# Second product of a fused feed-forward layer on four 32-row tiles of the tensor engine instead of the whole array

## The chip, the core and the metric

The kernel runs on one core of one Trainium2 chip. The core has a tensor engine (PE) with a queue of its own for instructions, a vector engine (DVE), a scalar engine (ACT), a general engine (POOL) and a sync engine (SP) that issues transfers; sixteen DMA engines carry the transfers. Matmuls write into eight banks of PSUM, each 128 partitions by 512 float32; DVE and ACT move results from there to SBUF. The metric is the device time of the program in microseconds (us), lower is better.

## What is computed

Attention with 32 learned queries, then attention of all tokens back to those 32 vectors, then a feed-forward layer with a leaky activation. B = 4 batches, N = 12480 tokens each, C = 128, m = 32, 2048 hidden units, 49920 tokens in all.

```python
def _attn_ref(x, inducing):
    B, N, C = x.shape                      # (4, 12480, 128)
    scale = 1.0 / np.sqrt(C)
    I = np.broadcast_to(inducing[None], (B, m, C))
    def mab(q, kv):
        s = scale * (q @ kv.transpose(0, 2, 1))
        a = np.exp(s - s.max(-1, keepdims=True))
        a /= a.sum(-1, keepdims=True) + 1e-09
        return a @ kv
    h = mab(I, x)                          # (B, 32, 128)
    return mab(x, h)

def _moe_ref(x, w_in, w_out, alpha):       # x: (49920, 128), d_ff = 2048
    h = x @ w_in
    g = np.maximum(h, 0.0) + alpha * np.minimum(h, 0.0)
    return g @ w_out
```

## The kernel before

**Algebra.** The output of the second attention is a weighted mean of the 32 rows of h, so the kernel never forms it. For each batch it makes hW = h times w_in (32 by 2048) once, and the hidden layer of a token is its 32 exponentials times hW, without the denominator, which is positive and goes through the activation. The leaky activation is split: g = relu(.) (1 - alpha) + alpha (.), so the output is relu(e hW) times W1 plus e times hA, with W1 = (1 - alpha) w_out and hA = h (w_in alpha w_out), 32 by 128. The division by the sum of exponentials comes last.

**Tiling.** A batch has six supertiles of 2048 tokens and a rest of 192. A supertile has four groups of 512 tokens; a batch has NG = 25 groups, the last of 192 tokens. For a group, the exponentials `rep` stand as 32 rows by 512 tokens, copied four times down the 128 partitions.

**A step of the main loop (L796-802).** A group has four steps j. `fill` (L443) makes four chunks of 128 hidden units: four matmuls of 32 rows each (`rep`, `hW`), one on each quarter of the array's rows, into four banks of the ring. ACT or DVE then reads each bank, takes the relu and writes it as bf16 to `gt` (L466, L468); which engine takes which bank is settled beforehand by a search, `make_plan` (L724). Then `mm2` (L473) of the step before adds its four chunks into the group's accumulator: four matmuls over all 128 rows with weights `W1`. There are two accumulators and a ring of six banks. `linear` (L497) adds e times hA with one more 32-row matmul for each group. `finish` (L507) turns a finished accumulator with DVE (L516), scales it by the denominators on POOL (L518) and stores it with four transfers from POOL's queue (L531), of the last groups from SP's. Every instruction of an engine is pinned to the order in which the program gives it (`pin`, L57).

**What is woven in.** `tasks` holds, by group and step, the work of the same batch's next supertile and of the next batch: `b_scores` (the exponentials of a supertile: four matmuls, one exp on ACT, a store to DRAM from SP), `b_rep` (four loads from SP that copy them), `b_den` and `b_turn` (denominators); for the next batch `a_load` (x by POOL's queue), `a_xpose` (a transposing transfer from SP, three groups later), `a_scores` (five groups after the load) and `a_accum` (eight groups after), one supertile every two groups; and at the batch's end `h_sum`, `h_den`, `h_transpose`, `h_weights` and `h_linear`. All of it uses banks of the ring. `h_weights` makes hW as 32 rows by 512 columns in four column quarters, and one DVE instruction moves it.

Of the kernel before, what the change touches and what calls it, by code (L numbers as in the profile page):

```python
# [16 lines left out]
P = 128  # L17
# [4 lines left out]
RING = 6  # L22
# [3 lines left out]
def kernel(  # L26
# [47 lines left out]
    xn_pool = ctx.enter_context(tc.tile_pool(name="xnp", bufs=8))  # L74
    xt_pool = ctx.enter_context(tc.tile_pool(name="xtp", bufs=2))
    gt_pool = ctx.enter_context(tc.tile_pool(name="gtp", bufs=4))
    head_pool = ctx.enter_context(tc.tile_pool(name="headp", bufs=3))
    rd_pool = ctx.enter_context(tc.tile_pool(name="rdp", bufs=3))
# [8 lines left out]
    )  # L87
    ring = [psum.tile([P, GRP], f32, name=f"ring{i}") for i in range(RING)]
    accs = [psum.tile([P, GRP], f32, name=f"acc{i}") for i in range(2)]
    ring_n = [0]  # L90

    def bank():
        t = ring[ring_n[0] % RING]
        ring_n[0] += 1
        return t
# [8 lines left out]
    def new_batch(b):  # L104
        st = Batch()
        st.b = b
        st.xT = xt_pool.tile([C, NS, NQ, GRP], bf16, name="xT", tag="xT")
        st.xTr = xt_pool.tile([C, JR, PR], bf16, name="xTr", tag="xTr")
        st.xn = {}
        st.e1T = {}  # L110
        st.sc = scale
        st.rs = None
        st.e2 = {}
        st.d = {}
        st.rep = {}
        st.rden = {}
        st.rt = {}
        if b > 0:
            st.es = work.tile([P, NS + 1], f32, name="es", tag="es")
            st.hacc = work.tile([P, C], f32, name="hacc", tag="hacc")  # L120
            nc.vector.memset(st.es[:], 0.0)
            nc.vector.memset(st.hacc[:], 0.0)
        return st

# [18 lines left out]
    def a_xpose(st, u):  # L143
        xn = st.xn[u]
        if u < NS:
            pin(nc.sync.dma_start_transpose(  # L146
                out=st.xT[:, u, :, :].rearrange("c q (j p) -> c (q j) p", j=NB),
# [8 lines left out]
    def p_xpose(st, u, i, last=False):  # L156
        xn = st.xn[u]
        if u == NS:
            tp = bank()[:].bitcast(bf16)
# [6 lines left out]
            ))  # L166
            return
        cut = 2 if last else 1
        for h in range(cut):
            tp = bank()[:].bitcast(bf16)  # L170
# [7 lines left out]
            dst = st.xT[:, u, qs[0] : qs[-1] + 1, :].rearrange("c q t -> c (q t)")  # L178
            w = len(qs) * GRP
            if h == 0:  # L180
                pin(nc.vector.tensor_copy(out=dst, in_=tp[:, :w]))  # L181
            else:
                pin(nc.scalar.copy(out=dst, in_=tp[:, :w]))

    def p_blocks(st, u, i):
        if u == NS:
            return [(st.xTr[:, j, :], st.xn[u][:, j, :]) for j in range(JR)]
        return [
            (st.xT[:, u, q, j * P : (j + 1) * P], st.xn[u][:, q, j * C : (j + 1) * C])
# [3 lines left out]
    def p_scores(st, u, i):  # L193
# [9 lines left out]
        ))  # L203
        st.e1T[u, i] = e1t
# [20 lines left out]
    def warm(st, n=1):  # L225
        for _ in range(n):
            mm(
                accs[0][:, P:], ident[:],
                st.xT[:, 0, 0, : 3 * P], start=False, stop=False, skip_group_check=True,
# [7 lines left out]
    def p_scale(st, et):  # L237
# [4 lines left out]
        pin(nc.vector.reciprocal(out=st.rs[:], in_=ps[:, 0:1]))  # L242

# [22 lines left out]
    def a_scores(st, u):  # L266
        ps = bank()
        if u < NS:
            for q in range(NQ):
                mm(ps[32 * q : 32 * q + 32, :], IT[:], st.xT[:, u, q, :])  # L270
# [3 lines left out]
            ))  # L274
            e1T = work.tile([P, NB, P], bf16, name="e1T", tag="e1T")
            pin(nc.sync.dma_start_transpose(out=e1T[:], in_=e1[:]))
        else:
# [5 lines left out]
            ))  # L283
            e1T = work.tile([P, JR, M], bf16, name="e1Tr", tag="e1Tr")
# [5 lines left out]
    def a_accum(st, u):  # L290
# [3 lines left out]
        if u < NS:  # L294
# [10 lines left out]
            ))  # L305
        else:
# [7 lines left out]
            ))  # L314

# [5 lines left out]
    def h_den(st):  # L321
# [5 lines left out]
        pin(nc.vector.tensor_scalar_mul(out=st.fr[:], in0=fold[:], scalar1=rh[:]))  # L327


    def h_transpose(st):  # L330
# [3 lines left out]
        pin(nc.vector.tensor_copy(out=st.hT4[:], in_=ps[:, :P]))  # L334
        st.hT = st.hT4[:, 0:M]

    def h_weights(st, first=False):
        ps = bank()
        for r in range(4):
            mm(  # L340
                ps[32 * r : 32 * r + 32, :], st.hT,
                w_in_b[:, r * NJ * P : (r + 1) * NJ * P],
            )
        st.hW = work.tile([P, NJ, P], bf16, name="hW", tag="hW")

        for j0, j1 in ((0, 1), (1, NJ)) if first else ((0, NJ),):
            evac_h(
                st, st.hW[:, j0:j1, :].rearrange("m j k -> m (j k)"), ps[:, j0 * P : j1 * P]
            )

    def h_linear(st):
# [3 lines left out]
        evac_h(st, st.hA[:], pa[:, :C])  # L355


    def tokens_of(st, s, q):
        return st.xT[:, s].rearrange("c j (q p) -> c j q p", q=NQ)[:, :, q, :]
# [4 lines left out]
    def b_scores(st, s):  # L364
# [14 lines left out]

        nq = NQ if s < NS else 1  # L380
# [14 lines left out]
    def b_scores_pe(st, q):  # L395
# [7 lines left out]
        ))  # L403
        st.rep[q] = st.rep0[:, q, :]

    def b_den(st, s):
# [11 lines left out]
        ))  # L418
        rt = dram.tile([pp, n, nq], f32, name="rt", tag="rt" if s < NS else "rtr")
# [15 lines left out]

    held = []

    def flush():
        while held:
            finish(*held.pop())  # L440

    def fill(st, g, j):
        pp, nb, cp = shape_of(g)  # L443
        t = pp * nb
        w = t * cp
        rep = st.rep[g]
        gt = gt_pool.tile([P, 4, GRP], bf16, name="gt", tag="gt")
        banks = []
        for r in range(4):
            ps = bank()  # L450
            for i in range(cp):
                mm(
                    ps[:, i * t : (i + 1) * t],
                    st.hW[32 * r : 32 * r + 32, j * cp + i, :],
                    rep[32 * r : 32 * r + 32, :t],
                )
            banks.append(ps)
        lin = j == NJ // cp - 1 and lin_groups(st.b, g)
        if lin:
            linear(st, lin)  # L460
        bits, pos = plan[st.b * NG + g, j]
        for r, ps in enumerate(banks):
            if r == pos:
                flush()
            if bits >> r & 1:
                pin(nc.scalar.activation(out=gt[:, r, :w], in_=ps[:, :w], func=RELU))  # L466
            else:
                pin(nc.vector.tensor_relu(gt[:, r, :w], ps[:, :w]))  # L468
        flush()
        return gt  # L470

    def mm2(st, g, j, gt):
        pp, nb, cp = shape_of(g)  # L473
        t = pp * nb
        acc = accs[(st.b * NG + g) % 2]
        begun = (g % 2 == 1 and st.b + g > 1) or cp > 1
        for r in range(4):
            for i in range(cp):
                c = r * NJ + j * cp + i
                mm(  # L480
                    acc[:, :t], W1[:, c, :], gt[:, r, i * t : (i + 1) * t],
                    start=(j == 0 and r == 0 and i == 0 and not begun),
                    stop=False, skip_group_check=True,
                )
        if j == NJ // cp - 1 and st.b * NG + g > 0:
            held.append((st, g))

    def lin_groups(b, g):
        if g % 2 == 0 and (b, g) != (0, 0):
            return [g, g + 1] if g + 1 < NS * NQ else [g]
        return []

    def linear(st, groups):
        for r, g in enumerate(groups):  # L497
            pp, nb, cp = shape_of(g)
            t = pp * nb
            mm(  # L500
                accs[(st.b * NG + g) % 2][:, :t], st.hA[32 * r : 32 * r + 32, :],
                st.rep[g][32 * r : 32 * r + 32, :t],
                start=(r == 1 or cp > 1), stop=False, skip_group_check=True,
            )

    def finish(st, g):
        pp, nb, _ = shape_of(g)  # L507
        t = pp * nb
        acc = accs[(st.b * NG + g) % 2]
# [6 lines left out]
        pin(nc.vector.transpose(out=ot[:, :t], in_=acc[:, :t]))  # L516
        ob = ob_pool.tile([P, GRP], f32, name="ob", tag="ob")
# [5 lines left out]
        t0 = st.b * N + s * SUP  # L523
# [312 lines left out]
```

## Time and profile before

| what | value |
|---|---|
| median of 3 runs (lowest, highest) | 590.22 us (589.33, 590.91) |
| the profiled execution, its own time | 591.21 us |
| its span | 589.4 us |
| granted tensor engine clock, mean over the span | 0.992 |
| PE busy (matmuls) | 558.5 us, 95% |
| DVE busy | 517.6 us, 88% |
| ACT busy | 502.0 us, 85% |
| POOL busy | 384.8 us, 65% |
| first `fill` of the main loop starts | 25.1 us |
| first turn of an accumulator (L516) | 38.9 us |
| last turn of an accumulator | 580.95 us |

The profile is one execution, on its own clock from the span's start. A row of groups names a line, an engine, an operation and out<-in by the program's names, then how often, the busy time, the mean duration of one, and the idle time of the engine before it with what ended that. A line of `L98` is the helper that records every matmul, so matmuls are told apart by their tiles. In a timeline the columns are start, duration and then the same names, and like instructions that follow each other closely are one row with their count. PE's matmuls overlap each other, and their durations hold a latency after the last column has streamed: the spacing of starts tells what one costs.

### The profile page before, as it was taken

How to read it: one execution, taken by the hardware profiler on the slowest of the kernel's cores; microseconds unless marked ns; L12 is line 12 of the kernel's file. 1: busy time of each engine (PE TensorE's matmuls, PEld its weight loads, DVE VectorE, ACT ScalarE, POOL GpSimd, SP SyncE). 2: the span in 40 equal slices, each digit the busy share in tenths (PEclk: the TensorE clock that was granted, in tenths of full speed). 3: DMA queues.
4: the chain of work that ended last, by engine and by line, in shares of the span. 5: the costliest groups of instructions: out<-in, count | busy, mean ns of one | idle time of the engine just before them, and what ended most of it. 6: DMA issues, size and time to landing. Idle time of an engine off the chain costs nothing.

```text
span 589.4 us, 12415 instructions
## 1 busy us (share of the span) xinstructions
PE 558.5 (95%) x4185; PEld 196.4 (33%) x4255; DVE 517.6 (88%) x869; ACT 502.0 (85%) x987; POOL 384.8 (65%) x558
## 2 busy tenths in 40 slices
PE   4999999999999999989999999999999999999994
PEld 4633333333333333323333333333333333333331
DVE  3689998999989999968989899899988999999993
ACT  2589888898899998968889989888889999999993
POOL 6658776667577766745667776756666766676651
PEclk9999999999999999989999999999999999999998
DMA  9958888952448779964246787896233333333322
GB/s 196 213 116 154 163 142 173 171 135 51 84 88 164 154 125 192 132 145 109 48 95 126 138 160 151 167 175 136 48 74 87 88 86 83 77 90 90 60 58 44
DMA packets 112640, 70.53 MB, mean 120 GB/s; under 512 B 86672, under 2 KB 102400, under 8 KB 112576
## 3 DMA queue, kind: packets, MB, share of 16 engines
q0 software_dynamic: 17232, 38.53, 33.3%
q1 hardware_dynamic: 95200, 30.69, 27.1%
q8 instruction: 33, 0.54, 0.4%
q10 hardware_dynamic: 144, 0.52, 0.3%
q14 instruction: 31, 0.25, 0.2%
HBM read 41.00 MB, written 28.95 MB: 119 GB/s over the span
## 4 chain that ended last, share of the span: by engine, by line
POOL 42%; issue 24%; PE 20%; DMA 9%; SPq 3%; ACT 0%; POOLq 0%; DVE 0%
POOL out_dram L531 28%; PE acc L98 13%; POOL ob L518 13%; PE ring L98 6%; DMA xT<-xn 3%; DMA xn<-in_x_dram 3%; DMA rdT<-rt 2%; POOL xn L132 1%; SPq L430 1%; SPq L146 1%; SPq L531 1%; DMA out_dram<-ob 0%; ACT gt L466 0%; DMA rt<-rd 0%; POOLq L531 0%
## 5 line engine op out<-in xcount | busy, mean ns | idle before, releaser
L466 ACT ACTIVATE gt<-ring 128x512 bf16<-128x512 f32 x899 | 469.4, 598 | 59.8 <-PE ring L98 26.9
L468 DVE TENSOR_SCALAR gt<-ring 128x512 bf16<-128x512 f32 x669 | 433.9, 685 | 45.9 <-PE ring L98 40.2
L98 PE MATMUL acc<-gt,W 128*128 128x512 bf16 x1530 | 391.2, 376 | 10.1 <-issue 8.9
L531 POOL DMA_DIRECT2D out_dram<-ob x384 | 245.8, 668 | 35.6 <-POOL ob L518 29.7
L518 POOL TENSOR_TENSOR ob<-ot,rdT 128x512 f32<-128x512 f32 (+1 forms) x100 | 105.5, 1055 | 152.9 <-DVE ot L516 146.3
L98 PEld LDWEIGHTS <-W 128*128 128x128 bf16 x1600 | 124.7, 98 | 173.1 <-issue 80.0
L98 PE MATMUL ring<-rep,hW 32*128 32x512 bf16 (+1 forms) x1600 | 159.1, 379 | 0.0
L98 PEld LDWEIGHTS <-hW 32*128 32x128 bf16 x1600 | 41.0, 91 | 166.0 <-issue 165.2
L516 DVE STREAM_TRANSPOSE ot<-acc 128x512 f32<-128x512 f32 (+1 forms) x100 | 69.4, 694 | 3.8 <-PE acc L98 3.8
L98 PE MATMUL acc<-rep,hA 32*128 32x512 bf16 (+1 forms) x100 | 19.3, 369 | 0.0
L132 POOL DMA_DIRECT2D xn<-in_x_dram x28 | 17.5, 634 | 2.6 <-DMA xn<-in_x_dram 1.8
L200 ACT ACTIVATE e1t<-ring 128x256 bf16<-128x256 f32 (+1 forms) x13 | 4.8, 372 | 9.8 <-PE ring L98 9.7
L272 ACT ACTIVATE e<-ring 128x512 bf16<-128x512 f32 x18 | 10.9, 603 | 1.9 <-PE ring L98 1.9
L181 DVE COPY xT<-ring 128x1024 bf16<-128x1024 bf16 (+1 forms) x12 | 8.0, 670 | 4.7 <-PE ring L175 4.2
L98 PE MATMUL ring<-xT,IT 128*32 128x512 bf16 x72 | 7.4, 401 | 3.9 <-DMA xT<-xn 3.9
L375 ACT ACTIVATE e<-ring 128x512 bf16<-128x512 f32 x18 | 10.9, 607 | 0.0
L98 PE MATMUL ring<-xT,hT 128*32 128x512 bf16 (+1 forms) x98 | 10.3, 389 | 0.0
L175 PE MATMUL ring<-ident,xn 128*128 128x128 bf16 x96 | 8.4, 242 | 1.4 <-DVE xn L630 0.9
L98 PEld LDWEIGHTS <-hT 128*32 128x32 bf16 (+1 forms) x122 | 3.7, 92 | 12.3 <-issue 12.2
L98 PE MATMUL ring<-xn,e1T 128*32 128x128 bf16 x288 | 7.3, 221 | 0.0
L98 PEld LDWEIGHTS <-e 128*128 128x128 bf16 x96 | 4.0, 96 | 9.4 <-issue 9.4
L175 PEld LDWEIGHTS <-xn 128*128 128x128 bf16 x96 | 6.5, 109 | 1.8 <-DVE xn L630 1.0
(85 smaller groups left out, 113.2 us busy)
## 6 DMA issues: line engine op xcount, KB each, us to landing
out_dram<-ob POOLq DMA_DIRECT2D x372, 64.0 KB, 2.7
rep<-e2d SPq DMA_DIRECT2D x92, 128.0 KB, 3.8
xn<-in_x_dram POOLq DMA_DIRECT2D x18, 512.0 KB, 6.0
e2d<-e SPq DMA_DIRECT2D x24, 128.0 KB, 1.9
xn<-in_x_dram POOLq DMA_DIRECT2D x10, 256.0 KB, 8.6
rdT<-rt SPq DMA_DIRECT2D x96, 8.0 KB, 2.7
w_out_f<-in_moe_w_out_dram POOLq DMA_DIRECT2D x4, 256.0 KB, 11.2
out_dram<-ob SPq DMA_DIRECT2D x12, 64.0 KB, 2.2
```

The source lines that it names most:

```text
L98: return pin(nc.tensor.matmul(o, lhsT, rhs, start=start, stop=stop, **kw))
L132: pin(nc.gpsimd.dma_start(out=xn[:, i * w : (i + 1) * w, :], in_=src[:, i * w : (i + 1) * w, :]))
L146: pin(nc.sync.dma_start_transpose(out=st.xT[:, u, :, :].rearrange("c q (j p) -> c (q j) p", j=NB), in_=xn[:].rearrange("p q f -> p (q f)"),))
L175: pin(nc.tensor.transpose(tp[:, k * P : (k + 1) * P], xn[:, q, j * C : (j + 1) * C], ident[:]))
L181: pin(nc.vector.tensor_copy(out=dst, in_=tp[:, :w]))
L272: pin(nc.scalar.activation(out=e1[:], in_=ps[:], func=EXP, scale=scale, accum_out=st.es[:, u : u + 1]))
L375: pin(nc.scalar.activation(out=e2[:].rearrange("p (t j i) -> p t j i", j=n, i=32), in_=turned(ps[:pp, :w], n), func=EXP, scale=scale_of(st ...
L466: pin(nc.scalar.activation(out=gt[:, r, :w], in_=ps[:, :w], func=RELU))
L468: pin(nc.vector.tensor_relu(gt[:, r, :w], ps[:, :w]))
L516: pin(nc.vector.transpose(out=ot[:, :t], in_=acc[:, :t]))
L518: pin(nc.gpsimd.tensor_tensor(out=ob[:, :t].rearrange("p (k m c) -> p k m c", k=nb, c=32), in0=ot[:, :t].rearrange("p (k m c) -> p k m c", ...
L531: pin((nc.sync if ending else nc.gpsimd).dma_start(out=dst[a], in_=ob[32 * a : 32 * a + 32, :t].rearrange("p (b k) -> p b k", k=32),))
```

## The change

The second product of most groups is no longer made with 128-row matmuls. A chunk's product is cut in four pieces of 32 rows (32 of its 128 hidden units), and each piece is a matmul on one quarter of the array's rows, which the code calls a tile. All 16 chunks of a group pass tile 0 first, with their first 32 rows, then all 16 pass tile 1 with the next 32 rows, and so on; between two tiles a semaphore, set behind the last piece on one tile, is waited for ahead of the first piece on the next, so that two tiles never add into the group's bank at once. At most three groups (`LANES`) are in flight, each on a tile of its own; a tile that holds no group takes `fill` matmuls, now one chunk at a time on whichever tile is free. So `h_weights` makes all 16 chunks of hW on all four row quarters: four full matmuls into four banks, and four moves. Up to 65 finished chunks wait in SBUF (`KEPT`). Eight banks are one pool: one for each group in flight, the rest for fills and tasks.

The order of PE's instructions, and which engine drains which bank, come from a clock that the program keeps while it is written (`clk`, `drained`), in place of the search. 92 of the 100 groups go this way; the first two groups, the last two full ones and the four of 192 tokens keep 128-row products (`whole`). Tasks with a matmul run at a pause: the start of certain groups, when all tiles have been let finish. `a_load` is now four groups and `a_xpose` two groups ahead of `a_scores`, and supertiles come mostly in pairs every four groups. The x tiles get fewer buffers (8 to 6) and transposed x is kept per supertile (8 tiles in place of two whole batches).

```diff
-RING = 6
+NBANK = 8
+LANES = 3
+KEPT = 66
...
+SLOT = 217
+XTS = 8
+DONE = 460
+SWITCH = 110
...
+    def drained(t, engine, ns, pe=0, after=190):
+        clk.pe += pe
+        start = clk.pe + after
+        if engine == "A":
+            clk.act = end = max(clk.act, start) + ns
+        else:
+            clk.dve = end = max(clk.dve, start) + ns
+        i = number[id(t)]
+        clk.free[i] = end + 170
+        idle.append(i)
...
+    def h_weights(st):
+        st.hW = hw_pool.tile([P, KC, P], bf16, name="hW", tag="hW")
+        for j in range(NJ):
+            ps = bank()
+            mm(ps[:], st.hT4[:], w_in_b[:, j * GRP : (j + 1) * GRP])
+            dst = st.hW[:, j * NJ : (j + 1) * NJ, :].rearrange("m j k -> m (j k)")
+            if st.rs is None and j % 2:
+                pin(nc.scalar.copy(out=dst, in_=ps[:]))
+                drained(ps, "A", 490, 220)
+            else:
+                evac_h(st, dst, ps[:])
+                drained(ps, "D", 620, 220)
...
+        after = 206 + w * 0.42
+        ca, cd = 52 + w * 0.83, 74 + w * 1.04
+        ready = clk.pe + after
+        if max(clk.act, ready) + ca <= max(clk.dve, ready) + cd:
+            pin(nc.scalar.activation(out=gt[:, :w], in_=ps[:, :w], func=RELU))
+            drained(ps, "A", ca, after=after)
+        else:
+            pin(nc.vector.tensor_relu(gt[:, :w], ps[:, :w]))
+            drained(ps, "D", cd, after=after)
+        seen[ch] = gt, clk.free[number[id(ps)]]
+
+    def piece(ch, i, rows=slice(0, P)):
+        b, g, u = ch
         pp, nb, cp = shape_of(g)
         t = pp * nb
...
+        return add(b, g, W1[rows, u * cp + i, :], seen[ch][0][rows, i * t : (i + 1) * t])
...
+        every = [(b, g) for b in range(B) for g in range(NG)]
+        direct = every[:2] + [(b, NG - 1) for b in range(B)] + every[-3:-1]
+        laned = [y for y in every if y not in direct]
...
+                for u, k in zip(order, when):
+                    k += base
+                    at(k + 4, lambda n=n, u=u: a_accum(states[n], u))
+                    at(k, lambda n=n, u=u: a_scores(states[n], u))
+                    at(k - 2, lambda n=n, u=u: a_xpose(states[n], u))
+                    at(k - 4, lambda n=n, u=u: a_load(states[n], u))
...
+                    if f == 0 and queue and sum(map(bool, tile)) + len(moving) < LANES:
+                        ch = (*queue[0], 0)
+                        if ch in seen:
+                            t = max(free_at[f], seen[ch][1] - 100 - SLOT)
+                            best.append((t, 2, f, "start"))
+                    if opening:
+                        best.append((free_at[f], 2, f, "open"))
+                    if fillable():
+                        t = max(free_at[f], min(clk.free[i] for i in idle) - 40)
+                        best.append((t, 4 + (f in taken), f, "fill"))
...
+                if pause(T0 + m):
+                    clk.pe = max(clk.pe, max(free_at) + SWITCH)
+                    for ch in wholes[m]:
+                        whole(ch)
+                    flush()
+                    run_tasks(T0 + m)
+                    clk.pe += SWITCH
+                    free_at = [clk.pe] * 4
...
+            if what == "enter":
+                x = next(x for x in moving if x[1] == f)
+                moving.remove(x)
+                tile[f] = [x[0], list(range(KC))]
+                pin(nc.tensor.wait_ge(fence, fences[x[0], f]))
+                continue
...
+                    piece(ch, 0, rows)
+                    spent(*y, 1)
+                    if f == 3:
+                        seen.pop(ch)
+                    if not todo:
+                        tile[f] = None
+                        if f < 3:
+                            pin(nc.tensor.drain(fusable=True)).then_inc(fence, 1)
+                            fenced += 1
+                            fences[y, f + 1] = fenced
+                            moving.append((y, f + 1, clk.pe + DONE))
+                        flush()
```

## The prediction

> **What bounds the kernel now.** I read first the page's busy times and costliest groups, to see which engine has no slack; then PE's timeline of a group without tasks, to see what its time is made of; last the transfers that tasks wait for.
>
> ```profile
> PE 558.5 (95%) x4185; PEld 196.4 (33%) x4255; DVE 517.6 (88%) x869; ACT 502.0 (85%) x987; POOL 384.8 (65%) x558
> ...
> L466 ACT ACTIVATE gt<-ring 128x512 bf16<-128x512 f32 x899 | 469.4, 598 | 59.8 <-PE ring L98 26.9
> L468 DVE TENSOR_SCALAR gt<-ring 128x512 bf16<-128x512 f32 x669 | 433.9, 685 | 45.9 <-PE ring L98 40.2
> L98 PE MATMUL acc<-gt,W 128*128 128x512 bf16 x1530 | 391.2, 376 | 10.1 <-issue 8.9
> ```
>
> PE is hardly ever idle, and ACT and DVE mostly wait for PE: PE sets the pace, with ACT and DVE close behind.
>
> ```profile
> 500.74 0.40 PE L98 MATMUL ring<-rep,hW 32*128 32x512 bf16 x4
> 501.07 1.04 PE L98 MATMUL acc<-gt,W 128*128 128x512 bf16 x4
> 502.04 0.40 PE L98 MATMUL ring<-rep,hW 32*128 32x512 bf16 x4
> 502.36 1.04 PE L98 MATMUL acc<-gt,W 128*128 128x512 bf16 x4
> 503.33 0.40 PE L98 MATMUL ring<-rep,hW 32*128 32x512 bf16 x4
> ```
>
> A step takes 1.295 us. Four full products end 1.04 us after the first starts, one alone takes 0.38 to 0.39, so they start 0.215 to 0.22 apart. The fills' four run side by side: 0.40 together. From products to fills is 0.97 = 4 x 0.215 + 0.11; from fills to products 0.32 = 0.215 + 0.105. So 0.215 us a step is spent on changing between whole array and row quarters. A group is four steps and half a pair of `linear`:
>
> ```profile
> 499.21 0.70 DVE L516 STREAM_TRANSPOSE ot<-acc 128x512 f32<-128x512 f32 x1
> 504.45 0.71 DVE L516 STREAM_TRANSPOSE ot<-acc 128x512 f32<-128x512 f32 x1
> ```
>
> 5.24 us. From the first turn (38.9) to the last product (580.6) are 541.7 us: 94 full groups of 5.24 make 492.6, four small ones of about 2.5 (two packs at 1.25 apart) 10, and 39 are left for tasks.
>
> **The change, term by term.**
>
> *Groups in flight.* Of 81 quarter matmuls of a group (64 pieces, 16 fills, `linear`) four run at once: 81 / 4 x 0.215 = 4.35 us if tiles never idle. But three groups in flight bind sooner. A group passes 65 matmuls on one tile at a time: 61 spacings of 0.215 (13.12) and three passes. A pass is a completion seen through a semaphore; the nearest row is ACT's start behind a pack (503.33 to 503.80): 0.45 to 0.47. With 3 x 0.45: 14.47, a third of it 4.82. On entering a tile a group can also meet a fill there: 0 to 0.215 at each of four entries, so up to 5.11; half of it gives 4.97. 92 groups x (4.97 - 5.24) = -25 us, bounds -39 and -12.
>
> *Evictions.* ACT's relus start 0.48 apart (two take 1.08, the last 0.60 of it), DVE's 0.60 to 0.61 (two take 1.29, the last 0.69), and a turn holds DVE 0.69 (504.45 to the next relu at 505.14). 16 relus and a turn balance at 0.48 a = 0.606 (16 - a) + 0.69: a = 9.6, 4.6 us; with the tasks' exps, sums, moves and small groups about 4.95. So they hide behind 4.97 and the pauses, barely. If a bank is late, PE's queue stops, and with it the pieces of all three groups, as the queue is one. The row for that is a pack that waited:
>
> ```profile
> 300.66 0.60 PE L98 MATMUL ring<-rep,hW 32*128 32x512 bf16 x4
> ```
>
> 0.60 in place of 0.40. The written clock gives a turn 606 ns where the trace has 690, so DVE falls behind it by 0.08 a group. None to one such hold a group: 0 to +18 us; I take +9.
>
> *Ramp.* When no group is left to start, the last runs out alone: two thirds of 14.47, +9.6. The last three groups' fills are made there, so their products follow bare: 32 x 0.215 + 16 x 0.081 = 8.2; three small ones at pauses 1.3 each. Before, these six were 2 x 5.24 + 4 x 2.5 = 20.5; now 12.1: -8.4.
>
> *Tasks and pauses.* By rows a `b_scores` costs 0.33 between a pack and products, `b_den` 0.12; inside a pause, in one mode, four column matmuls cost about 0.22. A batch of `b_scores`, `b_den`, `a_scores`, `a_accum` and the end work with four full matmuls for hW comes to 7.3, the last to 2.6: 24.5 of PE in place of 39, which held waits too. Some 36 pauses each cost two mode changes and on average half a slot until all tiles end, 0.11 + 0.105 + 0.108 = 0.32: +11.6. Together -3 if tasks cost PE their rows alone, +12 if they still bunch evictions as now. I take 0, nearer to the rows. hW's first moves are four on DVE instead of two: +1.
>
> *Transfers.* `a_xpose` goes to SP two supertiles at a time, two groups (9.9 us) ahead of the scores; loads two at a time from POOL's queue, 9.9 us before that, behind the stores of the group just ended.
>
> ```profile
> xn<-in_x_dram POOLq DMA_DIRECT2D x18, 512.0 KB, 6.0
> ...
> L146 SPq DMA_TRANSPOSE xT<-xn x18: 1335/3821/6277, 43.7 to 396.5; - x18
> ...
> DMA to landing us min/median/max: 4.3/7.7/10.7
> 253.15 0.62 PE L98 MATMUL ring<-xT,IT 128*32 128x512 bf16 x4 [2.34 <-DMA xT<-xn]
> ```
>
> The second lands a median issue (3.8) and landing (7.7) later: 11.5, so 1.6 late, for some eight heavy pairs 13 us; where no load runs beside them (the fastest: 4.3 to landing) none is late. The worst: a whole issue late, 30. I take +6. PE waits in a pause with all tiles empty, so nothing covers it; behind it on SP stand the next exponentials' store and copies, which fills need about 1.5 groups (7.5 us) after `b_rep` and which take 5.6 (four issues, 1.8, and 3.8 to landing).
>
> *The fence.* Folded into the last piece, the drain costs nothing but the pass priced above. The trace's records hold one drain of PE behind products, the last: it ends 293 ns after the last product starts, which streams 81. Left in the queue, each of 276 would empty the array for at least 0.21: +58 us. I take nothing, since the code marks it as one that may be folded.
>
> *Sum:* -25 + 9 + 9.6 - 8.4 + 0 + 1 + 6 = -7.6 on a span of 589.4. That execution took 591.2; against the median of 590.2 it gives **583 us**. A measurement tells 0.3% (1.8 us) from no change: 588.4 and 592.0.
>
> **Two rules weighed.** The pages here speak against the change more than the rows do. First row: eight fill matmuls of the small group, two on each tile in program order, take 0.35 (578.62), that is 0.081 + 0.08 + latency: the second on tile 0 does not hold back the first on tile 1.
>
> ```profile
> 578.62 0.35 PE L98 MATMUL ring<-rep,hW 32*128 32x192 bf16 x8
> ...
> 10.52 0.27 PEld L98 LDWEIGHTS <-xn 128*128 128x128 bf16 x8
> ```
>
> The Trainium skill ("TensorE: Matmul & The Clock Gate", "The mechanism") has matmuls start and end in strict program order; by it every fill out of step would hold the other tiles up to half a slot, an estimate of 16 x 0.1 us a group, and the change would lose. I take the row. Second row: eight full weight loads in 0.27 us, some 25 ns each, where the change needs 81 in 4.97 us, 61 ns each. The same page ("LDWEIGHTS (loading the stationary operand)") gives 128 columns / 1.2 ns, about 107 ns each; one after another, 8.6 us a group, by which the sum would be 920 us. I take the row here too.
>
> **Rivals.**
>
> 1. *Late banks hold the common queue: slower.* Place: the fills between pieces. For it: evictions need 4.95 of 4.97, and a fill is queued 40 ns ahead of its bank by a clock that prices a turn too short. Against: 65 finished chunks can wait, and pauses let evictions catch up. Price 0.35 us a group, 32 us in place of 9: 606. It decides from 0.18 a group (590).
> 2. *All fits: much faster.* Entries meet no fill, no bank is late, transfers land in time: -14, -9, -3: 557. For it: before, PE saw only 3.9 us of late transposes. Against: the thin slack of every part.
> 3. *The drain stays:* 583 + 58 = 641 at least. For it: the last piece may already carry an increment. Against: the folding mark.
> 4. *The tiles don't run side by side,* so the change does not do what it says: 64 pieces one after another, 13.8 us a group, beyond 1300. Against: the packs of 0.40.
>
> **How the numbers follow.** Forecast 0.42 (its own range 570 to 597: 0.30 below 588.4, 0.05 within, 0.07 above); late banks 0.34; all fits 0.16; drain 0.06; serial 0.02. Faster 0.30 + 0.16 = 0.46, same 0.05, slower 0.07 + 0.34 + 0.06 + 0.02 = 0.49. Cases of both signs are near even, since the new limits stand within 5% of the old. All bounds at their good end give 550, at their bad end 641. From 556 to 620 leaves out the drain, the serial case and a part of late banks above, and a little below.
>
> **What would show it.** Right: between pauses L516 starts 4.9 to 5.1 apart, most piece rows 0.215 apart on each tile, 81 loads a group, PE waiting little, pauses of 1 to 2 us. Late banks: idle time of PE, or of ACT and DVE waiting for it, and spacing beyond 5.3. Late transfers: waits of PE for `xT` of microseconds every fourth group. A drain that stays: 276 more of PE's sequencer records, all tiles stopping together three times a group. I am wrong altogether if turns come every 4.6 us, or if matmuls on other tiles stop while one waits for its own.

## The result, and the profile after

The kernel after the change takes 661.11 us (median of 4 runs, 654.83 to 664.31), beside 589.78 for the kernel before on the same chip: a ratio of 1.1199, 95% interval 1.1107 to 1.1291. Forecast were 583 and a range of 556 to 620. The profiled execution took 654.83, its span is 653.1, and its granted clock is 0.956 where before had 0.992. Ratios leave disturbed executions out, so one can lie a little beside the quotient of two medians.

The page of after, with the rows that answer to those of before (busy times, clock in 40 slices, the costliest groups with the idle time ahead of them):

```profile
PE 584.0 (89%) x8671; PEld 284.1 (43%) x8671; DVE 494.2 (76%) x849; ACT 506.6 (78%) x1018; POOL 385.9 (59%) x558
...
PEclk9996999999799997999989999799999999999878
...
L533 ACT ACTIVATE gt<-bank 128x512 bf16<-128x512 f32 (+1 forms) x924 | 468.9, 626 | 89.0 <-PE bank L126 86.3
L126 PE MATMUL bank<-gt,W 32*128 32x512 bf16 (+2 forms) x6016 | 532.0, 383 | 0.1
L536 DVE TENSOR_SCALAR gt<-bank 128x512 bf16<-128x512 f32 (+1 forms) x644 | 404.9, 680 | 118.3 <-PE bank L126 114.5
L126 PE MATMUL bank<-rep,hW 32*128 32x512 bf16 (+1 forms) x1600 | 416.8, 375 | 34.4 <-DMA rep<-e2d 26.1
```

PE's share of the span falls from 95% to 89%. ACT and DVE, which should have become the near bound, wait longer for PE than before (89 and 118 us in place of 60 and 46). The pieces almost never wait (0.1 us); the fills wait 34.4 us, most of it for the copies of the exponentials. The clock row has sixes and sevens in the middle of the loop, where before had nines and one eight:

```profile
PEclk9999999999999999989999999999999999999998
```

The view of waits says for what PE waited in after (engine and line, what it waited for: us in total, times, longest):

```profile
PEld L126 <- DMA rep<-e2d: 34.5, 10, 6.2
PE bank L126 <- DMA rep<-e2d: 29.7, 8, 5.7
...
PEld L126 <- DMA xT<-xn: 12.8, 3, 6.8
...
PE bank L126 <- DMA xT<-xn: 11.6, 2, 6.5
...
PE bank L126 <- DVE gt L536: 1.0, 3, 0.4
...
PE bank L126 <- ACT gt L533: 0.2, 1, 0.2
```

A wait shows twice, at the weight load and at the matmul, so each pair counts once. For evictions by DVE and ACT, the late banks of the prediction, the view lists 1.2 us of PE's waiting in the whole run (it lists waits of over 0.15 us in which no matmul runs). Between the starts of one matmul and the next there are nine gaps of over 2.5 us: seven ahead of matmuls that read `rep` (6.07, 5.89, 5.18, 4.81, 3.97, 3.28, 2.56) and two ahead of scores that read `xT` (6.93, 5.70), 44.4 us in all. One of them in PE's timeline (start, duration, engine, line, operation, count, and idle time with its releaser):

```profile
249.31 0.37 PE L126 MATMUL bank<-rep,hW 32*128 32x512 bf16 x1
249.46 0.40 PE L126 MATMUL bank<-gt,W 32*128 32x512 bf16 x3
255.38 0.60 PE L126 MATMUL bank<-rep,hW 32*128 32x512 bf16 x1 [5.52 <-DMA rep<-e2d]
255.38 1.89 PE L126 MATMUL bank<-gt,W 32*128 32x512 bf16 x12
```

One fill waits for `rep`; the pieces behind it don't read `rep`, and the first of them starts with the fill, twelve within 1.9 us. So the one queue held all four tiles. Why the copies came late is in SP's timeline of the same stretch; the pause with the scores was at 238.18:

```profile
239.91 0.34 SPq L469 DMA_DIRECT2D rt<-rd  x1
240.35 0.38 SPq L429 DMA_DIRECT2D e2d<-e  x1
240.82 3.17 SPq L317 DMA_TRANSPOSE e1T<-e  x2
244.10 2.48 SPq L479 DMA_DIRECT2D rdT<-rt  x4
246.63 3.09 SPq L437 DMA_DIRECT2D rep<-e2d  x4
```

The exponentials' store is issued at 240.35, the copies of it only at 246.63: two transposes and four copies of the denominators, which the same pause put there, stand between. The copies land at about 255.3; the first fill that reads them was next at 249.5. Four of the seven waits for `rep` (228.2, 255.4, 385.6 and 413.1) look like this, with 6.3 to 6.9 us between the issues of the store and of the copies. At 171.3 and 327.6, where a new batch begins, no transpose stands ahead:

```profile
160.26 0.38 SPq L429 DMA_DIRECT2D e2d<-e2r  x1
161.20 0.34 SPq L429 DMA_DIRECT2D e2d<-e  x1
161.65 1.83 SPq L479 DMA_DIRECT2D rdT<-rt  x4
163.57 4.96 SPq L437 DMA_DIRECT2D rep<-e2d  x8
```

Here the copies come 3.3 us after their store, and the one that PE waited for took 6.3 us to land (6.5 at 327.6), beside two loads of x; the median of all is 3.7. At 615.0, in the last batch, they come 3.5 us after it and land within 2 us.

What comes after such a wait is a second cost. Windows of 7 us, the first of each pair directly behind a gap of over 5 us, the second some 10 us later (busy time and count of each engine, then PE's granted clock, the DMA share and GB/s):

```profile
171.00:178.00 7.00, 6.63 (x76) 3.84 (x79) 3.48 (x6) 4.13 (x8) 0.00 (x0) 0.65 0.49 136
180.00:187.00 7.00, 6.88 (x105) 3.18 (x103) 4.31 (x8) 4.95 (x11) 4.17 (x7) 1.00 0.97 137
256.00:263.00 7.00, 7.00 (x74) 3.38 (x72) 2.19 (x4) 3.00 (x6) 0.00 (x0) 0.62 0.29 61
273.00:280.00 7.00, 7.00 (x118) 3.50 (x112) 5.41 (x10) 5.92 (x13) 4.25 (x6) 1.00 0.70 146
328.00:335.00 7.00, 7.00 (x84) 3.53 (x79) 4.58 (x8) 4.98 (x10) 1.07 (x1) 0.65 0.39 112
338.00:345.00 7.00, 7.00 (x119) 3.31 (x113) 5.89 (x11) 6.35 (x13) 3.27 (x5) 1.00 1.13 148
```

PE is busy in all six, but at a clock of 0.62 to 0.65 it runs 74 to 84 matmuls (mean 78), at full clock 105 to 119 (mean 114): a third fewer, some 2.2 us lost each time. The trace's record of the clock has it at half for 6.8 us around each of four long waits, for 13.65 around the two waits for `xT` that follow each other, and for 3.4 after the wait of 3.97; around the gaps of 3.28 and 2.56 it stays whole. That is 44 us, of which PE worked some 29, since the clock mostly fell before the wait was over; at 2.2 us for a long wait it costs some 13 us of time (an estimate). In the loop of before there is one such stretch, of 3.4 us, around a wait for `xT` of 2.7 us between starts.

### The profile page after: what moved, and what is told of

The parts are those of the page before. It is cut to its first block, busy times and chain, and to the rows that moved or that the text cites. A ratio compares the mean times of both kernels' runs of the same rounds, so it can differ in the third digit from the quotient of the medians.

```text
span 653.1 us, 20965 instructions
## 1 busy us (share of the span) xinstructions
PE 584.0 (89%) x8671; PEld 284.1 (43%) x8671; DVE 494.2 (76%) x849; ACT 506.6 (78%) x1018; POOL 385.9 (59%) x558
## 4 chain that ended last, share of the span: by engine, by line
PE 39%; POOL 18%; DMA 16%; issue 11%; ACT 7%; SPq 5%; DVE 3%; POOLq 0%; DVEq 0%; ACTq 0%
PE bank L126 39%; POOL out_dram L592 12%; DMA rep<-e2d 7%; ACT gt L533 6%; POOL ob L579 6%; SPq L479 3%; DMA xn<-in_x_dram 3%; DVE gt L536 2%; DMA xT<-xn 2%; DMA rt<-rd 1%; DMA e1T<-e 1%; SPq L437 1%; DMA rdT<-rt 1%; DMA out_dram<-ob 1%; DVE ot L576 1%
## 5 line engine op out<-in xcount | busy, mean ns | idle before, releaser
L533 ACT ACTIVATE gt<-bank 128x512 bf16<-128x512 f32 (+1 forms) x924 | 468.9, 626 | 89.0 <-PE bank L126 86.3
L126 PE MATMUL bank<-gt,W 32*128 32x512 bf16 (+2 forms) x6016 | 532.0, 383 | 0.1
L536 DVE TENSOR_SCALAR gt<-bank 128x512 bf16<-128x512 f32 (+1 forms) x644 | 404.9, 680 | 118.3 <-PE bank L126 114.5
L126 PE MATMUL bank<-rep,hW 32*128 32x512 bf16 (+1 forms) x1600 | 416.8, 375 | 34.4 <-DMA rep<-e2d 26.1
L126 PEld LDWEIGHTS <-W 32*128 32x128 bf16 (+1 forms) x6016 | 226.4, 94 | 220.2 <-issue 117.6
L126 PEld LDWEIGHTS <-hW 32*128 32x128 bf16 x1600 | 130.1, 92 | 84.0 <-issue 41.3
L576 DVE STREAM_TRANSPOSE ot<-bank 128x512 f32<-128x512 f32 (+1 forms) x100 | 69.1, 693 | 16.3 <-PE bank L126 16.2
L126 PE MATMUL bank<-rep,hA 32*128 32x512 bf16 (+1 forms) x100 | 36.3, 373 | 4.1 <-DMA rep<-e2d 3.6
L312 ACT ACTIVATE e<-bank 128x512 bf16<-128x512 f32 x18 | 10.6, 595 | 12.7 <-PE bank L126 12.0
L126 PE MATMUL bank<-xT,IT 128*32 128x512 bf16 x72 | 6.9, 407 | 12.1 <-DMA xT<-xn 11.6
L421 ACT ACTIVATE e<-bank 128x512 bf16<-128x512 f32 x18 | 11.2, 624 | 2.3 <-PE bank L126 2.1
L126 PE MATMUL bank<-xT,hT 128*32 128x512 bf16 (+1 forms) x98 | 10.4, 389 | 0.0
L126 PEld LDWEIGHTS <-IT 128*32 128x32 bf16 x75 | 2.5, 96 | 14.3 <-DMA xT<-xn 12.8
```

Source lines behind the costliest of these rows:

```text
L126: return pin(nc.tensor.matmul(o, lhsT, rhs, start=start, stop=stop, **kw))
L312: pin(nc.scalar.activation(out=e1[:], in_=ps[:], func=EXP, scale=scale, accum_out=st.es[:, u : u + 1]))
L421: pin(nc.scalar.activation(out=e2[:].rearrange("p (t j i) -> p t j i", j=n, i=32), in_=turned(ps[:pp, :w], n), func=EXP, scale=scale_of(st ...
L533: pin(nc.scalar.activation(out=gt[:, :w], in_=ps[:, :w], func=RELU))
L536: pin(nc.vector.tensor_relu(gt[:, :w], ps[:, :w]))
```

## The experiments

Theory T: late transfers, and the half clock behind them, cost about 60 us. Its rivals: D, drains that were not folded cost the most; B, late banks hold the common queue (the prediction's first rival). In the table's order, with ratios to the kernel before:

| label | us, median (runs) | ratio, 95% interval | clock |
|---|---|---|---|
| after | 661.11 (654.83 to 664.31) | 1.1199, 1.1107 to 1.1291 | 0.956 |
| no_rep_wait | 630.78 (626.19 to 644.87) | 1.0705, 1.0640 to 1.0771 | 0.964 |
| no_xT_wait | 655.20 (652.42 to 661.24) | 1.1125, 1.1049 to 1.1202 | 0.954 |
| no_wait | 599.56 (597.89 to 604.39) | 1.0181, 1.0122 to 1.0241 | 0.992 |
| all_drains | 721.45 (718.15 to 722.99) | 1.2228, 1.2170 to 1.2285 | 0.947 |
| fold | 651.23 (646.36 to 654.48) | 1.1005, 1.0925 to 1.1086 | 0.948 |
| kept50 | 640.06 (637.98 to 640.49) | 1.0837, 1.0778 to 1.0896 | 0.954 |
| rep_loads_early | 672.08 (670.97 to 676.49) | 1.1400, 1.1329 to 1.1471 | 0.937 |
| rep_loads_fold | 658.63 (642.66 to 666.76) | 1.0961, 1.0839 to 1.1083 | 0.948 |
| rep_fold | 640.14 (622.98 to 649.04) | none | 0.963 |
| rep_fold_k50 | 638.78 (630.09 to 656.45) | 1.0682, 1.0651 to 1.0712 | 0.962 |
| rep_spread_fold | 622.87 (613.72 to 634.14) | 1.0557, 1.0489 to 1.0625 | 0.971 |
| rep_spread_fold_k50 | 625.09 (620.76 to 628.80) | 1.0592, 1.0524 to 1.0660 | 0.967 |
| no_wait_fold | 592.98 (588.05 to 601.46) | 1.0028, 0.9988 to 1.0068 | 0.988 |
| transpose_resident | 666.20 (652.90 to 681.41) | 1.1141, 1.1035 to 1.1247 | 0.935 |
| no_load | 606.23 (603.01 to 616.28) | 1.0251, 1.0204 to 1.0299 | 0.990 |

### The waits taken away, one by one and together

`no_rep_wait` and `no_xT_wait` each have one half of this edit, `no_wait` both:

```diff
 fill, linear:
-                st.rep[g][32 * f : 32 * f + 32, :t],
+                w_in_b[32 * f : 32 * f + 32, :t],
 a_scores:
-                mm(ps[32 * q : 32 * q + 32, :], IT[:], st.xT[u][:, q, :])
+                mm(ps[32 * q : 32 * q + 32, :], IT[:], w_in_b[:, q * GRP : (q + 1) * GRP])
```

> The fills and the linear matmuls read w_in_b, a constant of the same shape, in place of the loaded exponentials rep; the transfers of rep still run, but no matmul waits for them. The output is therefore not the reference's. Theory T (late transfers and the clock that falls after a long wait): the profile after the change has 32 us of PE waiting for rep before fills and linear (2.6 to 6.1 us at a time), and half clock for 6.8 us behind the longer ones, worth up to 3.4 us each for five; so 661 falls to 610 to 630. Rival B (late banks): banks come no earlier, 650 or more. Rival D (60 drains that stayed): no change either.

> a_scores reads w_in_b in place of the transposed x of the next batch; the transposing transfers still run. The sums over the tokens are thereby wrong and with them the output. Theory T: two waits of 6.9 and 5.7 us at the start of the first batch and their 13.7 us at half clock go: 640 to 650. B and D: 655 or more.

> Both of these together: fills and linear read w_in_b in place of rep, a_scores reads it in place of transposed x. Theory T: 44 us of waits and some 24 us lost to the half clock go, 590 to 605, granted clock back to 0.98 or more, no half clock in the loop. B: 640 or more. D: 640 or more.

Without the wait for `rep` the kernel is 29 us faster (0.0494 x 590), without that for `xT` 4 us, without both 60 us. So `no_xT_wait` misses T's 640 to 650 and lies where B and D had it. The two don't add up, because each hides part of the other: in `no_rep_wait` the first batch's gaps ahead of the scores stay (3.8 and 5.4 us) and four of 2.2 to 2.9 appear later that after does not show, and in `no_xT_wait` there are nine waits for `rep` of 1.9 to 7.1. With both gone the clock row has no six or seven ahead of the last slices, and DVE waits for PE half as long. The page and the waits of `no_wait`:

```profile
PEclk9999999999999999999999999999999999999987
```

```profile
DVE gt L536 <- PE bank L126: 60.6, 82, 2.2
ACT gt L533 <- PE bank L126: 43.5, 68, 1.9
```

T stands with 60 us (interval about 54 to 67), of which 44 are the gaps themselves and some 13 the half clock. Either wait taken away alone gives much less than its share.

### The drains

```diff
 all_drains:
-                            pin(nc.tensor.drain(fusable=True)).then_inc(fence, 1)
+                            pin(nc.tensor.drain()).then_inc(fence, 1)
 fold (behind a fence, the next instruction is a piece that waits for nothing, if there is one):
-            t, _, f, what = min(best, key=lambda x: (max(x[0], clk.pe), x[1]))
+            quiet = [x for x in best if passed and x[2] and x[3] == "piece" and tile[x[2]][1][0]]
+            passed = False
+            t, _, f, what = min(quiet or best, key=lambda x: (max(x[0], clk.pe), x[1]))
...
                             fenced += 1
+                            passed = True
```

> The drains of the fence are not allowed to be folded into the matmul ahead: 276 drains in place of the 60 that the profile after the change shows. Each leaves about 0.50 us between starts of matmuls. Theory D (each empties the array for all three groups): 216 more at 0.2 to 0.3 us, 705 to 725, so that the 60 are worth 12 to 18 us of the loss. If the empty array is hidden by waits that come anyway (T): under 680.

> Edit: behind a fence, the planner's next instruction is a piece of another group that waits for nothing, where there is one; 19 drains stay in PE's queue in place of 60. T (late transfers and the half clock behind them cost about 60 us, drains little): 658 to 664, no difference. D (each drain that stays costs what the 216 added ones cost, 0.28 us): 41 fewer make -11, about 650, and the gaps of 0.5 us between starts of matmuls become fewer by about 40. B (late banks hold the queue): 661 or slower, since fills are moved out of the place that their banks set.

PE's records of after hold 63 drains, those of before 3: 60 of the 276 fences stayed in the queue, each where the last piece already carries an increment of PE's own semaphore. Keeping all 276 adds 0.1029 x 590 = 61 us for 216 drains, 0.28 us each. `fold` leaves 19 and is 0.0194 x 590 = 11 us faster than after, again 0.28 for each of 41. The second figure is rough: the interval of that difference is about 4 to 19 us, and its waits for `rep` and `xT` were no shorter (35.6 and 17.5 us). So the 60 of after cost about 17 us. D is right on the price and wrong as the main cause; T, which gave drains little, missed `fold` (658 to 664). B expected `fold` to be no faster, and fell here.

### Fewer kept chunks, and earlier transfers

```diff
 kept50:
-KEPT = 66
+KEPT = 50
 rep_loads_early:
-                at(t + 1, lambda b=b, s=s: b_rep(states[b], s))
+                at(t, lambda b=b, s=s: b_rep(states[b], s))
...
-                    at(k - 2, lambda n=n, u=u: a_xpose(states[n], u))
-                    at(k - 4, lambda n=n, u=u: a_load(states[n], u))
+                    early = b == 0 and k == base + 4
+                    at(k - 3 - 2 * early, lambda n=n, u=u: a_xpose(states[n], u))
+                    at(k - 6 - 2 * early, lambda n=n, u=u: a_load(states[n], u))
 rep_loads_fold: rep_loads_early and fold
```

> Edit: 50 finished chunks may wait in place of 66, so fills run about one group less ahead of the products and need rep about 4 us later; nothing else moved. T: the waits for rep shrink by up to 4 us each, most of about 32 us go, 630 to 645, clock 0.96 to 0.98. B (late banks hold the queue, fills run too close behind the evictions): slower than 661, with more waits for banks. Neither: 658 to 664.

> Edit: b_rep one pause earlier (directly behind b_scores), loads of x two groups and their transposes one group earlier, two more for the first batch. T (PE waits about 44 us for rep and xT, and has about 45 us of half clock behind that): the earlier issue takes most of the waits, 605 to 630, with a granted clock of 0.97 or more. If only the place of the wait moves (the DMA path itself is full): 650 to 665 at a clock of 0.95 to 0.96. D and B: the 17 us of drains and any late banks stay, so not below 600.

> Both edits: copies, loads and transposes earlier, and the piece behind a fence. T and D together: some 10 us below the same edits without the piece behind the fence, 595 to 620. If the waits have only moved: 640 to 655. It beats the kernel before (590) only if the waits go wholly and what else is left over the plan's 583 is under 7 us.

With 50 chunks kept the fills run one group less ahead and need `rep` later: its waits fall from 34.5 to 12.5 us and the kernel gains 21, within what T said; B expected the reverse. Waits for `xT` rose from 12.8 to 22.0, and the clock stayed at 0.954 where T had 0.96 to 0.98, so part of the 21 is not accounted for. `rep_loads_early` is a miss. The earlier copies did their part (waits for `rep` 3.0 us in all), yet the kernel became slower than after. The earlier loads and transposes, meant to end the waits for `xT`, raised them to 65.7 us, the longest 27.1. `rep_loads_fold` missed its 595 to 620 too: waits for `xT` of 47 us, and a ratio that stands for 647 us, what was expected if the waits had only moved. The DMA view of `rep_loads_early` for the stretch of 72 to 108 us (queues: packets, MB, share of the 16 engines; then issues with the median us to landing):

```profile
q1 hardware_dynamic: 4548, 1.14, 83.9%
q0 software_dynamic: 610, 1.71, 39.5%
...
xn<-in_x_dram POOLq DMA_DIRECT2D x2, 512.0 KB, 30.6
...
xT<-xn SPq DMA_TRANSPOSE x2, 28.9
```

The pair of transposes began on SP at 72.66, the two loads were issued at 72.84, and both took some 30 us instead of 8. So did POOL's stores in the stretch, with a median of 24.3 us to landing where the whole of after has 2.7. The packets of q1, which carries the transposes, took 83.9% of the engines' time while little was moved; shares of several queues can add up to more than 100%, as here, so they do not say that the engines were held.

### Where the loads and transposes stand

```diff
 rep_fold: b_rep at t, and fold; loads and transposes as in after
 rep_fold_k50: the same with KEPT = 50
 rep_spread_fold: rep_fold, and the transposes of a pair in two groups, each load two groups ahead of its own
+                    x = when[:i].count(k) - 3 - (b == 0 and k == 4)
...
-                    at(k - 2, lambda n=n, u=u: a_xpose(states[n], u))
-                    at(k - 4, lambda n=n, u=u: a_load(states[n], u))
+                    at(k + x, lambda n=n, u=u: a_xpose(states[n], u))
+                    at(k + x - 2, lambda n=n, u=u: a_load(states[n], u))
 rep_spread_fold_k50: the same with KEPT = 50, XTS = 10 and eight buffers of xn
```

> Edit: b_rep one pause earlier and the piece behind a fence; loads and transposes of x where the change has them. Now open: why loads and transposes two groups earlier made PE wait 64 us for xT. C (loads of x and transposes of x that run at the same time slow one another down, 27 to 31 us in place of 8): with them where they were, the waits for rep are gone (3 us, as with the earlier copies) and those for xT stay at 12 to 20 us in total: 625 to 635, clock 0.965 or more. W (the waits only move from one transfer to the next): 645 to 660.

> The same with 50 kept chunks. If what fewer kept chunks bring (21 us) is the later need of rep alone, it is gone here, where rep is early already: as with 66 chunks, within 5 us. If fewer kept chunks also let fewer fills run before a pause, so that something else is gained: 10 us or more below.

> As the first, and the two transposes of a pair in two groups (one and two groups behind the scores) with each load two groups ahead of its transpose, so that no load is issued with two transposes. C: the waits for xT shrink below 10 us in total, 605 to 622, clock 0.98. If the buffers of x are what holds loads and transposes (they are six and eight as in the change): waits for xT as with the earlier loads, 640 to 660.

> The same with 50 kept chunks and, in the room this leaves, eight buffers of loaded and ten of transposed x in place of six and eight. C: 595 to 615, some 5 us below the one before; with no waits at all and 19 drains left, 588, which is level with the kernel before. If buffers decide: clearly below the one before (20 us and more).

`rep_fold` tells little: its runs spread from 623 to 649, `rep` waits are down to 4.6 us, but those for `xT` are 34 us where C had 12 to 20. Fewer kept chunks bring nothing that shows here (638.8), which fits that in `kept50` they had mostly made `rep` be needed later, though the spread is as large as the 21 us in question. Spreading the transposes is the best that was found: waits for `xT` 8.7 us, for `rep` 5.9, 622.9 us, at the upper end of what C gave, and still 5.6% behind the kernel before. More buffers, in a run that also keeps fewer chunks, did not help (625.1, waits for `xT` 26.4), which speaks against buffers as what holds these transfers; C's 595 to 615 was missed.

### Whether loads slow transposes, and what is left without waits

```diff
 transpose_resident (on rep_loads_early): transposes of x from the second batch on
-                in_=xn[:].rearrange("p q f -> p (q f)"),
+                in_=w_in_b[:] if st.b else xn[:].rearrange("p q f -> p (q f)"),
 no_load: this, and from the second batch on
+                if st.b:
+                    xn = w_in_b[:].rearrange("p (q f) -> p q f", q=NQ)
+                    continue
                 pin(nc.gpsimd.dma_start(
 no_wait_fold: no_wait and fold
```

> The kernel with earlier copies, loads and transposes of x (672 us), but from the second batch on the transposes of x read rows that are resident, so they wait for no load; the loads run as before. The output is that of other scores. C (loads and transposes that run at the same time slow one another down): transposes of 15 us and more to landing stay, PE's waits for xT stay above 30 us, 645 to 672. L (the load alone was slow, the transpose only waited for it): transposes land in 4 to 9 us, waits for xT under 10 us, 615 to 630, while loads of 20 us and more stay.

> As the one before, and the loads of x from the second batch on are left out (the sums read resident rows too). C and L: transposes land in 4 to 8 us, waits for xT under 10 us, 605 to 625 at a clock of 0.97 or more. If the transposes are slow by themselves, for instance two in a row beside the stores: 15 us and more to landing stay, and 640 to 670.

> Left out: fills and linear read resident rows in place of rep, the scores resident rows in place of transposed x (as in the earlier run without either wait); with the piece behind a fence. D: 41 drains fewer, 0.28 us each, make -11 on that run's 600: 587 to 590, a granted clock of 0.99. If the drains only mattered where PE had waits before: 597 to 601.

The transposes' line, landing times in us (min, median, max), of `rep_loads_early`, then `transpose_resident`, then `no_load`:

```profile
DMA to landing us min/median/max: 4.4/6.8/34.6
```

```profile
DMA to landing us min/median/max: 4.3/8.1/34.9
```

```profile
DMA to landing us min/median/max: 4.4/7.4/12.7
```

PE's waits for them in `transpose_resident`, then in `no_load`:

```profile
PEld L126 <- DMA xT<-w_in_b: 73.3, 6, 31.9
```

```profile
PEld L126 <- DMA xT<-w_in_b: 5.7, 3, 2.1
```

Freed from the loads but beside them, transposes still take up to 34.9 us, and PE waits 73.3 us for them (in an execution of 681 us, the longest of the four); with the loads gone the slowest takes 12.7 and PE waits 5.7. So it is the two running side by side that makes them slow: C stands and L falls as the main cause. The ratio of `transpose_resident` lies 0.026 (15 us) under that of `rep_loads_early`, so a part for the order between them is not excluded. How the chip shares its DMA engines between them was not looked into.

`no_wait_fold` is level with the kernel before: 1.0028, 0.9988 to 1.0068. That is 9 us under `no_wait` for 41 drains, and it is what the scheme is worth when no transfer is late. No version that was run beats the kernel before, and this bound gives no reason to expect one from moving transfers alone.

## Why the prediction was wrong

*Groups in flight, evictions: right in sum.* Forecast were 4.97 us a group and 0.10 for late banks. In `no_wait`, the turns of the groups on the four tiles run from 58.8 to 577.7, 91 spacings in 518.9 us. Less 36 pauses of 44.1 us together (measured in after) and 60 drains of 0.28, a group is 5.03; the same working gives 5.05 in `no_wait_fold`. With its late banks the sum had 5.07. How the 5.03 divides is open: the view lists 1.2 us of waits for evictions in all of after where the sum had 9, but a hold shorter than it lists would count as part of the group. The sign that was named, turns 4.9 to 5.1 apart between pauses, is not there: single spacings run from 3.7 to 8.8, with a pause in them (mean 5.8) or without (5.7), so only the mean is explained, and how a group and a pause share it is a matter of this subtraction. Between the pieces themselves the rows are as taken: pieces of different tiles start a few ns apart and some 0.215 apart on each, fills among them, so rival 4 is wrong. So are the two rules that spoke against the rows: by their prices a group would take 6.6 or 8.6 us.

*Ramp and tail: about right.* The first of these turns comes 17.1 us after the last one of a whole product (41.7), where the forecast has a passage of 14.5 and a pause falls in between; from the last of them to the last product it is 9.7 where the bare products were to take 8.2.

*Tasks and pauses: 5 us too low.* The 36 pauses leave 44.1 us between pieces, 1.23 each. By the rows it was 11.6 + 24.5 = 36; the sum took no change, so the 39 of before. Within the bounds given (up to +12).

*Transfers: the step that failed.* The sum had +6, its bounds 0 to +30, for transposes that land 1.6 us late. It measured 60: of the 44 us of gaps in after the transposes' part is 12.6, and the copies for `rep`, with 31.8, were dismissed as needed 7.5 us after `b_rep` and taking 5.6. Those 5.6 were their own four issues and landing. The step left out what a pause puts ahead of them on SP (in the stretch shown, two transposes that together hold SP 3.17 us and four copies that hold it 2.48) and that they land in 6 to 7 us beside a load. So they came 6.3 us after the store was issued and then took 8.7, and fills were due before. At the start of a batch the slow landing beside the loads is enough. It had named SP's queue as the place to look, "behind it on SP stand the next exponentials' store and copies", and had not added the queue up for one pause. It also had no term for the half clock behind a wait, some 13 of the 60.

*Fence: taken at nothing, measured at 17.* The mark that a drain may be folded is not the folding. The third rival named the reason ("the last piece may already carry an increment") and was right for 60 of 276; its price, at least 0.21 each, measured 0.28.

*The sum again.* 583 - 6 (its transfers) + 17 + 5 (pauses) = 599, beside the 599.6 of `no_wait`; with the 60 of the transfers 659, beside the measured 661. That it meets so closely is partly luck, since the parts are known to a few us each. The first rival (late banks, 606) is excluded by the 1.2 us of waits for evictions that the view lists, by ACT and DVE waiting for PE and by `fold` and `kept50`; all fits (557) asked for transfers that land in time, and even `no_wait_fold`, where none is late, stands at 593 with its 19 drains.

## What to carry to other kernels

Where tasks are gathered into pauses, write out each queue's issues for one whole pause, in order and with durations, and set the end of each, with landing times from rows in which the same transfers run together, against the moment its first reader reaches the head of its own queue; an in-order queue with four independent streams is stopped by the one whose data is late. Price a wait of several microseconds at the wait and the slow clock behind it, and test suspected waits together as well as one by one. A fence that may be folded should be counted in the compiled instructions or in the trace, not taken as free.

## What the runs showed of the hardware

- Around each wait of 4.0 to 6.9 us in after, PE's granted clock fell to half, for 3.4 us after 3.97 and for 6.8 around a longer one; around gaps of 3.28 and 2.56 us it did not. There is no sharp limit in these runs: gaps of 2.9 us in `no_xT_wait`, 3.0 in `fold` and 2.7 in before brought 3.4 us of half clock. The changes of the clock in after lie whole multiples of 3.41 us apart, and behind each of these waits the clock came back after the first such step in which PE was busy from start to end. The Trainium skill ("TensorE: Matmul & The Clock Gate", "Part 1: The HAM clock gate") has the clock fall to half after one idle window of about 3.4 us and return after one busy window; the return in after agrees with that, while the fall came in three runs after shorter gaps as well.
- A drain left in PE's queue costs 0.28 us with four tiles busy, by 216 added (61 us); 41 removed (11 us, roughly) agree. One that may be folded stayed in the queue 60 times of 276 in after, each time behind a piece that increments PE's own semaphore.
- Transposes of x and loads of x by another queue slow one another down: some 30 us for two of each in `rep_loads_early`, where the median of all its transposes is 6.8 us, and at most 12.7 us for a transpose in `no_load`, where the loads are left out. The Trainium skill ("Advanced Engine Details and Errata", "X-Bar Transpose (TRN2)") says that transpose DMAs are as fast as regular ones; the medians to landing agree (in after 7.8 us for transposes of x and 7.6 for its loads of 512 KB), and the slowing side by side is beside what it states.
